# Attention worked in pairs of tiles, with k scaled behind the masks, gate sums behind the state products and expert 0's rows asked for earlier

## The chip, the cores and the metric

The kernel runs on one core of one Trainium2 chip. The metric is the device time of one launch in microseconds (us). The kernel before takes 944.06 us (median of 3 runs, 941.91 to 945.02).

## What is computed

Three layers follow one another. A causal attention with decay and without softmax runs over 4 sequences of 576 tokens, 8 heads of 64. A mixture of 8 experts, two per token, takes its output (2304 tokens of 512). A dense layer with a relu6 gate ends it.

```python
# attention, per head h:  gamma_h = 1 - 2**(-5-h)
scores = q @ k.T / sqrt(64)
ret    = scores * where(i >= j, gamma_h ** (i - j), 0)
x      = ret @ v                                     # (2304, 512)
# experts
noisy  = x @ w_gate + log1p(exp(x @ w_noise)) * noise
top2, weights = two largest of 8, softmax over the two
out[t] = sum over its two experts e of weight * relu(x[t] @ w1[e]) @ w2[e]
# dense
h = out @ w_in;  result = (h * clip(h + 3, 0, 6) / 6) @ w_out
```

## The kernel before

**Tiles.** The 2304 tokens are 18 tiles of 128 rows (`NT`), and a sequence is 4.5 tiles, so tile 4 of every nine (`m == 4`) holds the end of one sequence and the start of the next. The attention is linear in the past: a tile's output is the masked product of the tile with itself plus its queries times a state, the running sum of k^T v over the tiles before. One tile goes through these steps:

- `ks` (L196, VectorE) writes k divided by the decay at its position beside k; `qs` (L201, VectorE) scales the transposed q by a table.
- `tr` (L210, TensorE; L212, ScalarE) transposes the scaled k.
- `qk` (L226, TensorE) makes the scores of 8 heads in two PSUM banks, and VectorE multiplies each by the mask (L228, two instructions of 512 columns).
- `av` (L240) multiplies the state by q, `av2` (L250) adds the masked scores times v into the same PSUM tile `px`, and ScalarE copies `px` out in four pieces with a scale of its own for each (L267, eight pieces in tiles with `m == 4`).
- `kv` (L282) adds the tile to the state, and ScalarE copies the state out in one instruction (L284).
- `xt` (L294, L296) transposes the output back to rows for the scatter. For each three tiles `gsum` (L305, copy L307) makes the gate sums, `logit` (L313) folds them, and `route` turns them into slots.

**Order.** The order of every engine is written by hand; each engine runs its instructions in that order. The loop goes tile by tile: `xt(t-1)`, `tr(t+2)`, `av(t)`, `av2(t)`, `kv(t)`, then `ks` and `qs` of tile t+3, `qk(t+1)` with its masks, and `gsum` behind that. `route` is a generator; each `rstep()` runs one of its steps, five a tile. After its last step (L389) the slots of three tiles are known, and six scatters become ready.

**Scatter and rows.** Each `send` issues at most one scatter of a tile's rows to one of its two experts (a small spacer instruction, L412 or L414, and an indirect DMA, L415, both on GpSimd). `send` stands behind `tr`, `av2` and `xt`, so three a tile. At the end of tile 14 (`GA`) all scatters of tiles 0 to 11 (`EARLY` = 12) that are still open are issued at once, and `x_load` (L671) asks on the SP queue for expert 0's first 360 rows, which waits until every scatter has landed. In the last tile `x_tile` (L705) transposes these rows, and the first product of expert 0 (L738) follows the attention. Expert 0 runs in two sweeps (`si` 0 with 360 rows, `si` 1 with 256). In sweep 0 the rest of `route` and the last scatters run between the products; at its fifth step the slots are closed (`count`), the second load of expert 0's rows is asked for, and `fill` (L1265) marks unused slots of the other experts. Expert 1's rows are read (L683) behind the last `fill`, transposed by VectorE (L691), and expert 1 begins in sweep 2.

**PSUM.** The tag `acc` has five buffers, of which the state and the gate sums hold one each for good; `ga`, `gb` and `tp` have one each.

Of the kernel before, what the change touches and what calls it, by code (L numbers as in the profile page):

```python
# [7 lines left out]
F32 = mybir.dt.float32  # L8
F32R = mybir.dt.float32r
BF = mybir.dt.bfloat16  # L10
# [9 lines left out]
NT = N // 128  # L20
# [4 lines left out]
BZ = (7, 2)  # L25
# [12 lines left out]
C_ID, C_GK, C_GQ, C_MK, C_MM, C_IO, C_EB = 0, 128, 200, 272, 400, 528, 536  # L38
C_EC, C_FO, C_PI = 544, 552, 568
C_W = 569  # L40


def shape_consts():
    c = np.zeros((P, C_W + 320), np.float64)
    p = np.arange(P)
    c[:, C_ID:C_ID + P] = np.eye(P)
    le = (p[:, None] <= p[None, :]).astype(np.float64)
    c[:, C_MK:C_MK + P] = le
    c[:, C_MM:C_MM + P] = le * ((p[:, None] // 64) == (p[None, :] // 64))
# [4 lines left out]
    head = 2 * np.arange(4)[None, :] + (p // 64)[:, None]  # L54
    for m in range(9):
        c[:, C_GQ + m * 4:C_GQ + m * 4 + 4] = g[head] ** (m * P if m < 5 else m * P - S)
    c[:, C_GQ + 36:C_GQ + 40] = g[head] ** -64.0
# [22 lines left out]
class K:  # L80
# [32 lines left out]
    def consts(self):  # L113
        nc, cp, i = self.nc, self.cp, self.i
        nc.scalar.preload_act_table_set("natural_log_exp_and_others")
        self.c = cp.tile([P, C_W], F32, name="cst")
        nc.sync.dma_start(self.c[:, 0:C_MK], i["cst"][:, 0:C_MK])
        self.grow = self.big([P, 2048], BF)[0:6, 0:640]
        nc.gpsimd.dma_start(self.grow.bitcast(F32), i["cst"][0:6, C_W:C_W + 320])
        warm = self.row([P, 1024], BF)  # L120
        nc.vector.memset(warm, 0.0)
        self.warm = warm
        self.sbd = [self.row([P, 4, D]) for j in range(2)]
        self.ident = self.c[:, C_ID:C_ID + P]

    def table(self):

        nc = self.nc
        p = self.pacc([P, 512])
        nc.tensor.matmul(p, self.grow[:, 512:640], self.grow[:, 0:512], start=True, stop=True)  # L130
        self.gt = self.row([P, 512])
        nc.scalar.activation(self.gt, p, AF.Copy)

# [44 lines left out]
    def load(self, t, names="kqv"):  # L178
        nc, i = self.nc, self.i
        if t in self.raw:  # L180
            return self.load_of(t, names)
        kq = self.big([P, 2, H, D])
        vk = self.big([P, 2, H, D])
        self.raw[t] = dict(k=kq[:, 0], q=kq[:, 1], v=vk[:, 0], ks=vk[:, 1])
        self.load_of(t, names)
# [7 lines left out]
    def ks(self, t):  # L193
        m, r = t % 9, self.raw[t]
        gk = self.c[:, C_GK + m * 8:C_GK + m * 8 + 8]
        self.nc.vector.tensor_mul(r["ks"], r["k"], gk[:, :, None].to_broadcast([P, H, D]))  # L196
# [7 lines left out]
    def tr(self, t):  # L204
# [3 lines left out]
        sv = r["ks"].rearrange("p h d -> p (h d)")  # L208
        for a in range(4):
            nc.tensor.transpose(p[:, a, :], sv[:, a * P:(a + 1) * P], self.ident)  # L210
        r["kT"] = r["k"].rearrange("p h d -> p (h d)").rearrange("p (a i) -> p a i", a=4)
# [3 lines left out]
    def qk(self, t):  # L215
        nc = self.nc
        r = self.raw[t]
        mk = C_MM if t % 9 == 4 else C_MK
        mask = self.c[:, mk:mk + P]
        pt = self.big([P, 2, 4, P])  # L220
        p0 = self.ps.tile([P, 4, P], F32, name="sc0", tag="ga")
        p1 = self.ps.tile([P, 4, P], F32, name="sc1", tag="gb")
# [4 lines left out]
        for s, p in enumerate((p0, p1)):  # L227
            nc.vector.tensor_mul(pt[:, s], p, mask[:, None, :].to_broadcast([P, 4, P]))  # L228
        r["pt"] = pt

    def av(self, t):
        nc, m = self.nc, t % 9
        r = self.raw[t]
        px = (self.ps.tile([P, 2, P], F32, name="px", tag="tp"), self.pacc([P, 2, P]))
        n = 64 if m == 4 else P
        if m:
            for a in range(4):
                for u in range(2):
                    h, s = slice(u * 64, u * 64 + 64), u ^ a % 2
                    nc.tensor.matmul(px[a % 2][s * 64:s * 64 + 64, a // 2, :n], self.sbd[t % 2][h, a, :],  # L240
                                     r["qT"][h, a, :n], start=(a < 2), stop=False, skip_group_check=True)
        self.px = px

    def av2(self, t):
        nc, m = self.nc, t % 9
        r, px = self.raw[t], self.px
        for a in range(4):
            for s in range(2):
                h = slice(s * 64, s * 64 + 64)
                nc.tensor.matmul(px[a % 2][h, a // 2, :], r["v"][:, 2 * a + s, :], r["pt"][:, s ^ a % 2, a, :],  # L250
                                 start=(m == 0 and a < 2), stop=True, skip_group_check=True)
# [4 lines left out]
        w = self.c[:, C_GQ + m * 4:C_GQ + m * 4 + 4]  # L256
        if m == 0:
            for j in range(2):
                nc.scalar.activation(r["xT"][:, j::2], px[j], AF.Copy)
        elif t + 1 == NT:  # L260
            for j in range(2):
                nc.vector.tensor_mul(r["xT"][:, j::2], px[j],
                                     w[:, j::2, None].to_broadcast([P, 2, P]))
        else:
            n = 64 if m == 4 else P
            for a in range(4):
                nc.scalar.activation(r["xT"][:, a, :n], px[a % 2][:, a // 2, :n], AF.Copy, scale=w[:, a:a + 1])  # L267
                if m == 4:
                    nc.scalar.activation(r["xT"][:, a, n:], px[a % 2][:, a // 2, n:], AF.Copy, scale=self.c[:, C_GQ + 36 + a:C_GQ + 37 + a])
        self.send(r["xT"][:, 0])  # L270

    def kv(self, t):
# [7 lines left out]
        for h in range(H):  # L280
            a, s = divmod(h, 2)
            nc.tensor.matmul(self.pS[s * 64:s * 64 + 64, a, :], r["ks"][lo:, h, :], r["v"][lo:, int(HS[h]), :],  # L282
                             start=(m in (0, 4) and a == 0), stop=False, skip_group_check=True)
        nc.scalar.activation(self.sbd[(t + 1) % 2], self.pS, AF.Copy)  # L284

    def xt(self, t):
# [3 lines left out]
        if t == 0:  # L290
            self.pg = self.pacc([P, 512])
        p = self.pacc([P, 4, P])
# [6 lines left out]
    def gsum(self, g):  # L299

        nc = self.nc
        p = self.pacc([P, 3 * P])
# [6 lines left out]
    def logit(self, t):  # L309
        self.raw.pop(t)  # L310
        o = t % 8 * 16
# [5 lines left out]
    def route(self, g0, G):  # L317
        nc, sb, v = self.nc, self.sb, self.nc.vector
        lg = sb.tile([P, G, 16], F32, name="lg")
        for g in range(G):  # L320
            if g == 0 or (g0 + g) % 8 == 0:
                n = min(G - g, 8 - (g0 + g) % 8)
                o = (g0 + g) % 8 * 16
                v.tensor_copy(lg[:, g:g + n, :], self.pg[:, o:o + n * 16].rearrange("p (g e) -> p g e", g=n))
# [47 lines left out]
        o = 128 + g0 // 3 % 2 * 32  # L372
# [56 lines left out]
    def late_base(self):  # L429

        nc, cp, v = self.nc, self.cp, self.nc.vector
        p = self.pg[:, 192:200]
# [9 lines left out]
    def attention(self):  # L442
        self.raw, self.xrow, self.sq = {}, {}, []
        self.consts()
        self.load(0, "kq")
        self.load(1, "kq")
        self.nc.sync.dma_start(self.c[:, C_MK:], self.i["cst"][:, C_MK:C_W])
        self.load(0, "v")
        self.load(2, "kq")
        self.load(1, "v")  # L450
        self.load(3, "kq")
# [12 lines left out]
        self.tr(1)  # L464
        self.ks(2)
        self.qs(2)
        self.late_consts()
# [3 lines left out]
        for t in range(NT):  # L471
            if 0 < t < NT - 3:
                self.load(t + 3)
            if t in WL:
                self.w_load()
            self.rstep()

            if t:
                self.xt(t - 1)
                self.zero(t - 1)  # L480
            if 0 < t < NT - 2:
                self.tr(t + 2)
            if t and t % 3 == 0:
                self.gate(t - 1, groups)
            self.rstep()
            self.av(t)
            self.rstep()
            self.wstep(WM)

            self.av2(t)  # L490
            self.kv(t)
            if t == 0:
                self.tr(2)
            if t + 1 == NT:
                xs = self.x_new(0)
                self.x_tile(0, xs, 0, "acc")
                self.x_tile(0, xs, 1, "gb")
            self.rstep()
            if t + 3 < NT:
                self.ks(t + 3)  # L500
                self.qs(t + 3)

            if t + 1 < NT:
                self.qk(t + 1)
            if t % 3 == 2 and t + 1 < NT:
                self.gsum(t // 3)
            if t + 1 < NT:
                self.rstep()
# [7 lines left out]
            if t in WS:  # L516
                self.w_split()
            if t + 1 < NT:
                self.wstep(WN)
        self.gsum(NT // 3 - 1)  # L520
        self.x_tile(0, xs, 2, "tp")
        self.xt(NT - 1)
        self.gate(NT - 1, groups)
        self.rstep()
        self.wstep(WN)
# [915 lines left out]
```

## Time and profile before

| what | us |
|---|---|
| median of 3 runs | 944.06 |
| the profiled execution | 944.83 |
| its span, first to last instruction | 942.7 |
| TensorE busy in the span | 925.9 |
| VectorE busy | 612.6 |
| ScalarE busy | 466.4 |
| GpSimd busy | 238.5 |

The attention takes about the first 104 us of the span, the eight experts and the dense layer the rest. TensorE is busy 98% of the span. A profile gives for each instruction its start, its length and, where its engine was idle before it, what released it; lengths of TensorE instructions overlap, so a dense stretch is read from the distance of starts.

### The profile page before, as it was taken

To read this page: it belongs to the slowest core of one execution; us is meant where nothing else is said; L and a number is where in the kernel's file an instruction comes from. 1 tells how busy PE (TensorE), PEld (TensorE's weight loads), DVE (VectorE), ACT (ScalarE), POOL (GpSimd) and SP (SyncE) were. 2 spreads that over 40 slices of the span, in tenths; PEclk is the share of its full clock that TensorE was granted. 3 is DMA by queue.
4 is the path that set the end of the run, shared out by engine and by line. 5 is a ranking of instruction groups with operands and counts; after the bars stand their busy time and mean duration, and the time that the engine had idled before them with its cause. 6 is when DMAs were issued, how large, how long until landed. Compare 5 with 4: busy or idle time off the path is not lost.

```text
span 942.7 us, 17785 instructions
## 1 busy us (share of the span) xinstructions
PE 925.9 (98%) x6314; PEld 819.6 (87%) x6314; DVE 612.6 (65%) x1327; ACT 466.4 (49%) x1025; POOL 238.5 (25%) x324
## 2 busy tenths in 40 slices
PE   8998999999999999999999999999999999999997
PEld 6876888988888989888888888989999999899996
DVE  5776765887979888796866536645645554574442
ACT  4655543556464564645535435544545454445342
POOL 1246260433324242332500213033004212400000
PEclk9999999999999999999999999999999999999999
DMA  9963766767969788696657678778579676956541
GB/s 336 376 236 126 278 211 231 234 220 253 291 218 292 246 262 251 209 271 210 200 179 244 231 264 295 265 244 262 183 254 286 207 229 235 275 188 214 179 157 49
DMA packets 123742, 221.22 MB, mean 235 GB/s; under 512 B 13037, under 2 KB 60915, under 8 KB 123643
## 3 DMA queue, kind: packets, MB, share of 16 engines
q1 hardware_dynamic: 113819, 190.47, 61.6%
q0 software_dynamic: 9392, 28.73, 8.9%
q8 instruction: 52, 0.85, 0.4%
q10 hardware_dynamic: 432, 0.79, 0.2%
q14 instruction: 47, 0.39, 0.1%
HBM read 163.97 MB, written 55.97 MB: 233 GB/s over the span
## 4 chain that ended last, share of the span: by engine, by line
PE 87%; DVE 4%; DMA 2%; ACT 2%; issue 2%; POOL 1%; SPq 1%; another core or an unknown queue 0%; DVEq 0%; ACTq 0%; POOLq 0%
PE p L755 40%; PE ga L738 12%; PE gb L738 9%; PE mga L1167 7%; PE p L1167 5%; PE mgb L1167 2%; PE mtp L1167 2%; PE sc L226 2%; PE px L250 1%; DVE b L592 1%; PE p L294 1%; PE p L210 1%; PE p L282 1%; ACT b L591 1%; DMA xe<-s,free 1%
## 5 line engine op out<-in xcount | busy, mean ns | idle before, releaser
L755 PE MATMUL p<-b,h 128*120 128x512 f32 (+1 forms) x1056 | 261.0, 395 | 0.0
L755 PEld LDWEIGHTS p<-b,h 128*120 128x120 f32 (+1 forms) x1056 | 189.1, 185 | 41.5 <-DVE h L797 0.4
L755 PE MATMUL p<-b,b 128*128 128x512 f32 x768 | 180.0, 390 | 0.0
L755 PEld LDWEIGHTS p<-b,b 128*128 128x128 f32 x768 | 142.2, 188 | 28.2
L738 PE MATMUL ga<-x,b 128*128 128x360 f32 (+1 forms) x768 | 134.2, 323 | 2.1 <-DVE h L797 1.9
L738 PEld LDWEIGHTS ga<-x,b 128*128 128x128 f32 x768 | 124.8, 188 | 10.8 <-DVE h L797 6.4
L641 POOL TENSOR_TENSOR cvl<-cvl,cvs 128x256 f32<-128x256 f32 x64 | 50.4, 787 | 214.9 <-ACT cva L622 150.8
L592 DVE TENSOR_TENSOR b<-b,b 128x512 fp32r<-128x512 f32 x128 | 93.6, 766 | 13.9 <-ACT b L591 13.6
L738 PE MATMUL gb<-b,b 128*128 128x256 f32 x672 | 89.8, 282 | 0.1
L738 PEld LDWEIGHTS gb<-b,b 128*128 128x128 f32 x672 | 86.9, 190 | 1.4 <-DVE b L694 0.3
L884 POOL DMA_INDIRECT s<-yd,slotc x36 | 37.3, 1037 | 179.6 <-DVE b L1030 56.1
L591 ACT ACTIVATE b<-b 128x512 fp32r<-128x512 f32 x128 | 74.0, 625 | 0.0
L1205 DVE SCALAR_TENSOR_TENSOR b<-s,b 128x512 fp32r<-128x512 f32 x64 | 44.3, 693 | 44.9 <-ACT b L1204 40.5
L1204 ACT ACTIVATE b<-s 128x512 fp32r<-128x512 f32 x64 | 40.5, 632 | 59.3 <-DVE s L1202 53.1
L642 POOL TENSOR_TENSOR cvl<-cvt,cvl 128x256 f32<-128x256 f32 x64 | 59.2, 925 | 5.0
L1201 ACT ACTIVATE s<-s,three 128x512 f32<-128x512 f32 x64 | 45.8, 716 | 25.4 <-DVE s L1188 25.4
L1167 PE MATMUL mga<-b,b 128*128 128x256 f32 x384 | 56.2, 282 | 0.0
L797 DVE SCALAR_TENSOR_TENSOR h<-gb,h 128x256 fp32r<-128x256 f32 (+1 forms) x64 | 27.8, 434 | 43.4 <-PE p L755 30.6
L1188 DVE TENSOR_TENSOR s<-p,mc 128x256 f32<-128x256 f32 x32 | 13.6, 424 | 64.4 <-PE p L1167 64.0
L1167 PEld LDWEIGHTS mga<-b,b 128*128 128x128 f32 x384 | 52.6, 191 | 2.5
L1202 DVE SCALAR_TENSOR_TENSOR s<-s,s 128x512 f32<-128x512 f32 x64 | 44.0, 687 | 7.4 <-DMA paced<-s 4.6
L1172 ACT ACTIVATE mc<-mga 128x256 f32<-128x256 f32 x64 | 24.5, 383 | 48.3 <-PE mga L1167 47.1
(206 smaller groups left out, 1440.1 us busy)
## 6 DMA issues: line engine op xcount, KB each, us to landing
b<-wc SPq DMA_DIRECT2D x112, 512.0 KB
b<-in_moe_w_dram SPq DMA_DIRECT2D x64, 512.0 KB
wc<-b SPq DMA_DIRECT2D x32, 512.0 KB
s<-xe SPq DMA_DIRECT2D x140, 64.0 KB
s<-in_moe_w_in_dram SPq DMA_DIRECT2D x32, 256.0 KB
s<-in_moe_w_out_dram SPq DMA_DIRECT2D x32, 256.0 KB
b<-wc SPq DMA_DIRECT2D x32, 256.0 KB
yd<-s SPq DMA_DIRECT2D x24, 240.0 KB
```

Source lines behind the costliest of these rows:

```text
L591: self.nc.scalar.activation(h, a, AF.Copy)
L592: rest = lambda h=h, l=l, a=a: self.nc.vector.tensor_sub(l, a, h.bitcast(F32))
L641: nc.gpsimd.tensor_mul(lf, lf, s.bitcast(F32))
L642: nc.gpsimd.tensor_add(lf, t.bitcast(F32), lf)
L738: nc.tensor.matmul(p, a[k], b[:, k, :n], start=(i == 0), stop=(i == 11))
L755: nc.tensor.matmul(a[:R], x[:, c], y[:, fi, :], start=(first and i == 0), stop=(last and i == 2))
L884: nc.gpsimd.indirect_dma_start(out=r, out_offset=None, in_=self.yd[0:rows], in_offset=bass.IndirectOffsetOnAxis(ap=self.slotc[:, t, k:k + ...
L1167: nc.tensor.matmul(t, w[:, u, k], x[:, z, k], start=(first and i == 0), stop=(last and i == 5), skip_group_check=True)
L1201: nc.scalar.activation(r, x, AF.Relu, bias=self.three)
L1202: v.scalar_tensor_tensor(x, r, 6.0, x, op0=OP.min, op1=OP.mult)
L1204: nc.scalar.activation(h[:, 0], x, AF.Copy, scale=1.0 / 6.0)
L1205: v.scalar_tensor_tensor(h[:, 1], x, 1.0 / 6.0, h[:, 0].bitcast(F32), op0=OP.mult, op1=OP.subtract)
```

## The change

- The loop goes over pairs of tiles. In a pair t: `kv(t+1)`; `av2` of both tiles; one copy of both tiles' `px` for each of its two halves (`px_out`, ScalarE, without a scale; four copies where the two tiles fall in different groups of three); `kv(t+2)`; `qk` and masks of t+2 and t+3; `ks(t+3)`; `av` of t+2 and t+3; `gsum` if a group of three has ended; `xt` of t and t+1; `tr` of t+4 and t+5; `gate`; `qs` of both and `ks(t+4)`. Nine `rstep()`s stand in a pair.
- The decay between tiles is applied to the state where it is copied out (four ScalarE instructions of 64 columns with a scale each, instead of one of 256).
- `tr` transposes the raw k. `ks` then scales k in place, and the masks carry the factor (`dm`, made at the start by two VectorE instructions of 512 columns).
- The scores of odd tiles use the tag `acc`, the row transposes of `xt` the tags `ga` and `gb`; the gate sums share the bank of the logits.
- At the start the small table of decays is asked for on ScalarE's queue instead of GpSimd's, the order of the first loads is another, and the warming matmuls are 6, 4 and 2 instead of 7 and 2.
- The forced scatters and `x_load` stand at the start of pair 14, and the first two steps of the loop (tile 0's and 1's scores) stand ahead of it.

```diff
     def av(self, t):
+        if t % 2 == 0 or t == 1:
+            self.px = (self.ps.tile([P, 2, 2, P], F32, name="px", tag="tp"), self.pacc([P, 2, 2, P]))
...
+    def px_out(self, t):
+        for j in range(2):
+            if t % 3 == 2:
+                for u in (t, t + 1):
+                    nc.scalar.activation(self.raw[u]["xT"][:, j::2], self.px[j][:, u - t], AF.Copy)
+                continue
+            x = self.xg[t // 3][:, j::2, c:c + 2 * P].rearrange("p a (t i) -> p a t i", t=2)
+            y = self.px[j].rearrange("p t a i -> p a t i")
...
+                nc.scalar.activation(x, y, AF.Copy)
+        for u in (t, t + 1):
+            self.send(self.raw[u]["xT"][:, 0])
...
     def kv(self, t):
-        nc.scalar.activation(self.sbd[(t + 1) % 2], self.pS, AF.Copy)
+        w = C_GQ + (t + 1) % 9 * 4
+        for a in range(4):
+            nc.scalar.activation(self.sbd[(t + 1) % 2][:, a], self.pS[:, a], AF.Copy, scale=self.c[:, w + a:w + a + 1])
...
         self.busy(BZ[0])
         self.table()
-        self.ks(0)
         self.tr(0)
+        self.decays(0)
         self.qs(0)
-        self.ks(1)
+        self.decays(1)
+        self.busy(BZ[1])
         self.qs(1)
-        self.busy(BZ[1])
-        self.qk(0)
+        sc = self.qk(0)
         self.gate_w()
         self.tr(1)
+        self.ks(0)
+        self.masks(0, *sc)
+        self.busy(BZ[2])
+        sc = self.qk(1)
+        self.kv(0)
+        self.tr(2)
+        self.ks(1)
+        self.masks(1, *sc)
+        self.av(1)
+        self.tr(3)
...
+        for t in range(0, NT, 2):
+            last = t + 2 == NT
...
             if t == GA:
                 while self.sent < EARLY:
                     self.rstep()
                     self.send()
                 self.xr = {}
                 self.x_load(0, 0)
...
+            self.rstep()
+            self.kv(t + 1)
+            self.rstep()
+            self.av2(t)
+            self.av2(t + 1)
+            self.px_out(t)
+            if last:
+                xs = self.x_new(0)
+                self.x_tile(0, xs, 0, "acc")
+                self.x_tile(0, xs, 1, "gb")
+            else:
+                self.kv(t + 2)
+                self.rstep()
                 self.wstep(WN)
+                for u in (t + 2, t + 3):
+                    self.masks(u, *self.qk(u))
+                self.ks(t + 3)
+            self.rstep()
...
+            if not last:
+                self.av(t + 2)
+                self.av(t + 3)
+            if done:
+                self.gsum(g)
+            if last:
+                self.x_tile(0, xs, 2, "tp")
+            for u in (t, t + 1):
+                self.xt(u)
+                self.zero(u)
+            for u in (t + 4, t + 5):
+                if u < NT:
+                    self.tr(u)
+            if done:
+                self.gate(3 * g + 2, groups)
+            if t + 4 < NT:
+                self.qs(t + 4)
+                self.qs(t + 5)
+                self.ks(t + 4)
+            for _ in range(4):
+                self.rstep()
...
+            self.wstep(WN)
+            self.rstep()
```

## Rows read from the trace of the kernel before

**Rows 1.** The page's first part: busy time and share of each engine.

```profile
PE 925.9 (98%) x6314; PEld 819.6 (87%) x6314; DVE 612.6 (65%) x1327; ACT 466.4 (49%) x1025; POOL 238.5 (25%) x324
```

**Rows 2.** Busy time by stretch: window, length, engines, TensorE clock, DMA share, GB/s.

```profile
20.00:30.00 10.00, 10.00 (x174) 8.39 (x168) 6.15 (x15) 6.27 (x19) 0.00 (x0) 1.00 1.03 376
60.00:70.00 10.00, 9.15 (x144) 7.49 (x145) 9.62 (x36) 6.61 (x19) 3.65 (x6) 1.00 0.24 91
```

**Rows 3.** Chain of work to 200 us, pieces of TensorE: start us, us, what.

```profile
17.57 1.09 PE sc L226 x16
...
21.77 1.09 PE sc L226 x16
...
24.23 0.44 PE p L210 x4
...
25.84 0.37 PE px L250 x4
...
40.16 0.37 PE px L250 x4
...
54.97 0.37 PE px L250 x4
...
61.14 0.32 PE px L250
...
81.94 0.37 PE px L250 x4
```

**Rows 4.** Timeline of the start, TensorE, then VectorE: start us, us, instruction, [idle before].

```profile
1.48 3.17 PE L138 MATMUL p<-s 128*128 128x512 bf16 x7 [1.48 <-DVE s L121]
5.35 0.60 PE L130 MATMUL p<-b 6*128 6x512 bf16 x1 [0.70 <-DMA b<-in_cst_dram]
...
7.78 2.07 PE L226 MATMUL sc<-b 64*128 64x128 f32 x16
...
6.62 0.69 DVE L201 TENSOR_TENSOR b<-b,s 128x512 f32<-128x512 f32 x1 [1.77 <-ACT s L132]
```

**Rows 5.** Timeline of GpSimd's scatters, 74 to 91 us.

```profile
74.03 1.26 POOL L415 DMA_INDIRECT xe<-s,slots  x1 [0.15 <-issue]
...
78.74 1.25 POOL L415 DMA_INDIRECT xe<-s,slots  x1 [0.16 <-issue]
...
85.36 0.97 POOL L415 DMA_INDIRECT xe<-s,slots  x1 [0.22 <-issue]
...
90.86 0.97 POOL L415 DMA_INDIRECT xe<-s,slots  x1 [0.23 <-issue]
```

**Rows 6.** Timeline of SP's queue, then TensorE, around expert 0's first rows.

```profile
93.85 1.37 SPq L671 DMA_DIRECT2D s<-xe  x3
98.71 0.22 SPq L515 DMA_DIRECT2D paced<-s  x1
...
101.14 0.63 PE L705 MATMUL p<-cst,s 120*128 120x120 f32 x4
...
103.11 0.63 PE L705 MATMUL xp<-cst,s 120*128 120x120 f32 x4
...
104.60 0.58 PE L738 MATMUL ga<-x,b 128*128 128x360 f32 x2
```

**Rows 7.** Timeline of all engines, last scatters to the first product of expert 1.

```profile
117.77 0.97 POOL L415 DMA_INDIRECT xe<-s,slots  x1 [3.65 <-ACT h L796]
...
117.81 0.53 DVE L797 SCALAR_TENSOR_TENSOR h<-gb,h 128x360 fp32r<-128x360 f32 x1 [0.81 <-ACT h L796]
...
127.57 0.82 SPq L671 DMA_DIRECT2D s<-xe  x2
...
131.68 1.10 POOL L1265 DMA_INDIRECT xe<-s,free  x1 [5.79 <-DVE b L592]
...
150.79 0.73 DVE L691 STREAM_TRANSPOSE xp<-s 128x512 f32<-128x512 f32 x1 [2.70 <-DMA s<-xe]
...
160.70 2.25 PE L738 MATMUL ga<-x,b 128*128 128x360 f32 x12 [0.53 <-DVE h L797]
```

More of the change, by code (lines that the diff above doesn't have):

```diff
@@ L24 @@
 EARLY = 12
-BZ = (7, 2)
+BZ = (6, 4, 2)
 WL, WS = (9, 11, 13, 15), (10, 14)
@@ L217, in qk @@
         r = self.raw[t]
[L218 to L219 removed]
         pt = self.big([P, 2, 4, P])
[L221 to L222 removed]
+        p0, p1 = (self.pacc([P, 4, P]) if t % 2 else self.ps.tile([P, 4, P], F32, name="sc", tag=tag) for tag in ("ga", "gb"))
         for a in range(4):
@@ L226, in qk, with masks @@
                 nc.tensor.matmul(p[:, a, :], r["kT"][h, a, :], r["qT"][h, a, :], start=True, stop=True)
-        for s, p in enumerate((p0, p1)):
-            nc.vector.tensor_mul(pt[:, s], p, mask[:, None, :].to_broadcast([P, 4, P]))
-        r["pt"] = pt
+        return pt, (p0, p1)
+    def masks(self, t, pt, ps):
+        nc = self.nc
+        for s, p in enumerate(ps):
+            nc.vector.tensor_mul(pt[:, s], p, self.dm[:, s])
+        if t % 9 == 4:
+            nc.vector.memset(pt[0:64, :, :, 64:P], 0.0)
+        self.raw[t]["pt"] = pt
     def av(self, t):
@@ L233, in av @@
         r = self.raw[t]
-        px = (self.ps.tile([P, 2, P], F32, name="px", tag="tp"), self.pacc([P, 2, P]))
+        if t % 2 == 0 or t == 1:
+            self.px = (self.ps.tile([P, 2, 2, P], F32, name="px", tag="tp"), self.pacc([P, 2, 2, P]))
+        px = [x[:, t % 2] for x in self.px]
+        first = t % 2 == 0 or t % 9 == 1
         n = 64 if m == 4 else P
@@ L240, in av @@
                     nc.tensor.matmul(px[a % 2][s * 64:s * 64 + 64, a // 2, :n], self.sbd[t % 2][h, a, :],
-                                     r["qT"][h, a, :n], start=(a < 2), stop=False, skip_group_check=True)
-        self.px = px
+                                     r["qT"][h, a, :n], start=(first and a < 2), stop=False, skip_group_check=True)
     def av2(self, t):
         nc, m = self.nc, t % 9
-        r, px = self.raw[t], self.px
+        r, px = self.raw[t], [x[:, t % 2] for x in self.px]
         for a in range(4):
@@ L250, in av2 @@
                 nc.tensor.matmul(px[a % 2][h, a // 2, :], r["v"][:, 2 * a + s, :], r["pt"][:, s ^ a % 2, a, :],
-                                 start=(m == 0 and a < 2), stop=True, skip_group_check=True)
+                                 start=False, stop=True, skip_group_check=True)
         g = t // 3
@@ L255, in av2 @@
         r["xT"] = self.xg[g][:, :, t % 3 * P:t % 3 * P + P]
[L256 to L270, printed above, removed]
+    def px_out(self, t):
+        nc = self.nc
+        r, c = self.raw[t], t % 3 * P
+        for j in range(2):
[5 more added lines that the diff above has]
+            y = self.px[j].rearrange("p t a i -> p a t i")
+            if j and t + 2 == NT:
+                nc.vector.tensor_copy(x, y)
+            else:
+                nc.scalar.activation(x, y, AF.Copy)
+        for u in (t, t + 1):
+            self.send(self.raw[u]["xT"][:, 0])
     def kv(self, t):
@@ L319, in route @@
         lg = sb.tile([P, G, 16], F32, name="lg")
[L320 to L324, printed above, removed]
+        v.tensor_copy(lg, self.pg[:, 0:G * 16].rearrange("p (g e) -> p g e", g=G))
         yield
@@ L444, in attention @@
         self.consts()
[L445 to L451, printed above, removed]
+        for t, nm in ((0, "kq"), (1, "kq"), (0, "v"), (2, "k"), (3, "k"), (1, "v"), (2, "q"), (3, "q")):
+            self.load(t, nm)
+        self.nc.sync.dma_start(self.c[:, C_IO:], self.i["cst"][:, C_IO:C_W])
         self.load(2, "v")
@@ L470, in attention @@
         self.live, self.sent, self.xg = [], 0, {}
[L471 to L508, printed above, removed]
+        self.pg = self.pacc([P, 512])
+        for t in range(0, NT, 2):
+            last = t + 2 == NT
+            for u in (t, t + 1):
+                if u + 4 < NT:
+                    self.load(u + 4)
+                if u in WL:
+                    self.w_load()
             if t == GA:
```

64 lines of the change are left out of this document (32 added, 32 removed).

## The prediction, made before the changed kernel was run

> **What bounds the kernel now.** I read the page's busy shares first: TensorE has work for 925.9 of 942.7 us [rows 1]. So the change can gain only what TensorE idles in the attention: it moves the time at which the first product of expert 0 starts, 104.60 [rows 6], and any wait it makes later. Then the windows: at 20 to 30 us TensorE is full and VectorE has 6.15 of 10; at 60 to 70 VectorE is at 9.62 and TensorE falls to 9.15 [rows 2]. Then the chain, for distances. From the scores of one tile to those of the next (17.57 to 21.77) are 4.20: a plain tile. From `av2` of tile 3 (25.84) to that of tile 6 (40.16) are 14.32 [rows 3]: three tiles (12.6) and 1.7 for a group's gate sums, logits and routing. From tile 9 (54.97) to tile 10 (61.14) it took 6.17 [rows 3], 1.97 over a plain tile, in the stretch in which VectorE is full: `av2` waits for masks that have little other work ahead of them. Last I read GpSimd and SP, since slots, scatters and the request for rows form a chain beside TensorE.
>
> **Part A, the start.** Before, the decay table arrives at 5.35, after 0.70 of idle TensorE; `qs(0)` waits for it until 6.62 and the first scores start at 7.78 [rows 4]. On ScalarE's queue I expect it when six warming matmuls end (seven took 3.17): 1.48 + 6 x 0.45 = 4.2; at worst, if that queue is no faster, at 5.35 as before. The scores then wait for the transposed k and for up to four more warming matmuls (1.8 at the same pace): 6.8 to 7.3. The masks' factor, two VectorE instructions of 0.69 [rows 4], lies where VectorE waited for the table (1.77 idle there); without that cover it would cost 1.4. Now count to equal work: `qk(2)` begins at 17.57 [rows 3], behind the scores, masks and states of tiles 0 and 1. Of a plain tile's 4.20, `qk` is 1.09, `tr` 0.44 and `xt` about 0.5 [rows 3]; `av` is 0.6 (what lies from the end of `tr` to 25.84, less 0.6 for `logit`), so `av2` and `kv` are 1.6. Behind the first scores stand `qk(1)` 1.1, three `tr` 1.4, `av2` and `kv` twice 3.2, `av(1)` 0.6, two warming matmuls 0.5 and about 0.5 of waiting for the first state: 7.3. The first scores end at 7.9 (at 1.09) to 9.4 (at the 2.07 of [rows 4]), so this ends at 15.2 to 16.7, and `xt(0)`, 0.5, is still owed. Gain 0.4 to 1.9; I take 1.3.
>
> **Part B, the loop up to pair 14.** Every matmul stays. What goes is the wait of `av2` for masks, which now stand a whole pair ahead: 1.97 at tile 9 and, by the same subtraction at tiles 10 and 12, perhaps 0.7 more: 2.7. Fewer changes of matmul shape (eight a pair for twelve) may give another 0.1 a pair. What comes: VectorE's masks and scalings are eight instructions of at most 0.69 a pair, 5.5; where routing and weight splits come on top, two tiles fill VectorE with 9.6 [rows 2], as much as TensorE's 8.4 to 9.5 for a pair. There, in pairs 10 and 12, VectorE still binds and 0 to 2 come back. On ScalarE the copies of `px` fall from eight to two a pair and those of the state rise from two to eight; the trace shows no state copy with a scale, but in a pair they have the scores ahead of the next `av` as cover, 2.2; if ScalarE is late by more than that, each pair pays the rest. The odd tile's scores hold two `acc` buffers that `tr(t+4)` needs; `av`, `xt` and the even tile's masks lie between, about 1 us of room. `ks(t+4)` now waits for that `tr`; behind it on VectorE stand only routing steps. Sum: a gain of 2.5, between 4.4 and a loss of 0.5. With A, pair 14 starts 3.8 sooner. The same work (`kv(14)`, `qk(15)`, `av(15)`, `tr(17)` done) stands before at 81.94 [rows 3] plus 0.6 + 1.1 + 0.6 + 0.4 = 84.6; now 80.8.
>
> **Part C, from there to the first product of expert 0.** Before: 104.6 - 84.6 = 20.0. TensorE's own work in the new order is 8.4 + 1.3 - 0.9 = 8.8 for pair 14 (gate work added, no `tr`), 2.0 for the last two `av2`, then 101.14 to 104.60 [rows 6] and a second `xt`, 4.0: 14.8. It will not run so, since the rows come later. Counting routing steps (11 a group, nine a pair), the slots of tiles 6 to 8 are ready only at the end of pair 10, those of tiles 9 to 11 at the end of pair 12. So pair 12 issues six scatters and the start of pair 14 forces six more, back to back. GpSimd needs (78.74 - 74.03)/3 = 1.6 for one that waits for a tile's copy and (90.86 - 85.36)/4 = 1.4 for a forced one [rows 5]. Two go out before `xt(12)`; four follow from 1.2 ahead of pair 14 (5.3 at 1.3 each to 7.0), then six (8.2): the last ends 12.3 to 14.0 after pair 14 starts. Before, the last ended at 91.83 (90.86 + 0.97), the request followed 2.0 later (93.85), and the third tile of rows was there 4.8 after that (98.71) [rows 5, 6]. So now it is there at 19.1 to 20.8; its transpose, two `xt` and `logit` (103.11 to 104.60 [rows 6], and 0.5) end at 21.1 to 22.8. Against 20.0 that costs 1.1 to 2.8; I take 1.9. TensorE, ready for the rows at 10.8, would wait some 6. Asking sooner does not help: the scatters are what is late. SP is not: the fourth weight load now stands ahead of the request.
>
> **Part D, expert 1.** By the same count the last group's slots come at the first routing step of step 3 of sweep 0, not at the end of step 2. On VectorE that lies behind the instruction at 117.81, so its six scatters start near 119.3, not 117.77 [rows 7]. Behind them follow the second request of expert 0's rows (127.57), `fill` (131.68, which must not overtake that read), and expert 1's rows, for which VectorE waits 2.70 until 150.79 and TensorE 0.53 at 160.70 [rows 7]. So the chain has no slack: 1.6 goes in, of which VectorE may make up half over five tiles of rows. Cost 0 to 1.6; I take 0.8.
>
> **Sum.** -1.3 - 2.5 + 1.9 + 0.8 = -1.1 on the profiled 944.83. That execution is 0.8 over the median, so the median goes from 944.06 to 943.0. The four terms will not all fall on one side: 939.5 to 947 for this case.
>
> **Rivals.** (1) The rows are in time: the scatters do not queue as I count, and part C is 14.8 plus 1 of small waits, 4.2 less than before: -1.3 - 2.5 - 4.2 + 0.8 = -7.2, 937. For it: GpSimd is busy 3.65 of 10 at 60 to 70 [rows 2]. Against: twelve scatters at 1.4 to 1.6 need 18, two pairs. (2) Slower: a wait of 6 for the rows lowers TensorE's clock, and what follows runs at half speed. The granted clock reads 1.00 in both windows [rows 2], the level of 2.4 GHz; but the first scores took 2.07 for what takes 1.09 later [rows 3, 4], as at 1.2 GHz. The 4 behind the wait would take up to 4 more: 943.0 + 4 = 947. [...] The Trainium skill, "TensorE: Matmul & The Clock Gate" (Part 1), has the array start at 1.2 GHz and fall back to it when it has idled; the start agrees, and no wait of before is long enough to show the fall. (3) VectorE binds all pairs and B is a loss of 1.4: 946.9. For it: 9.62 at 60 to 70; against: 6.15 at 20 to 30 [rows 2].
>
> **How the numbers follow.** A difference under 0.3% (2.8) can't be told from none. Forecast 0.53, rival 1 0.19, rival 2 0.18, rival 3 0.10. Faster (below 941.2): rival 1 and 0.08 of the forecast's low end, 0.27. Slower (above 946.9): half of rivals 2 and 3 and 0.08 of the high end, 0.22. Same: 0.51. The range takes in the forecast's bounds, rival 3, most of rival 2 and the upper part of rival 1: 938.5 to 947.5.
>
> **What would show it.** After: the table before 4.5 and first scores near 7; no idle TensorE ahead of `av2`; ten scatters in a row around pair 14; a long idle stretch of TensorE ahead of the first transposes of expert 0's rows, ended by that load, with the first product near 102.7; doubled lengths behind it for rival 2. VectorE's first transpose for expert 1 stands 47 to 48 behind that product, not 46.2. I am wrong if TensorE goes through the last pair without a wait (rival 1), or if the pairs themselves stall.

## The result, and the profile after

The changed kernel takes 957.31 us (median of 4 runs, 956.41 to 958.46). The kernel before, run beside it on the same chip, takes 943.71 (941.91 to 945.02). The ratio is 1.0146, 95% interval [1.0126, 1.0167]: 13.6 us slower, where 943.0 was forecast and 947.5 was the upper end.

The profiled execution took 956.41, its span is 954.2. First the page's busy times, which answer [rows 1]:

```profile
PE 929.6 (97%) x6317; PEld 823.1 (86%) x6317; DVE 613.8 (64%) x1328; ACT 466.3 (49%) x1024; POOL 236.2 (25%) x323
```

TensorE's busy time rose by 3.7 only, the span by 11.5. Before, the first product of expert 0 started at 104.60 [rows 6]; now it starts at 115.20, 10.6 later, and behind it lie 839.0 where 838.1 lay before. So the loss is in the attention. The windows of that stretch, after (columns as in [rows 2]):

```profile
50.00:60.00 10.00, 8.14 (x98) 5.43 (x95) 4.16 (x9) 2.61 (x11) 4.60 (x8) 0.83 0.92 311
60.00:70.00 10.00, 8.29 (x118) 7.36 (x116) 4.94 (x26) 6.12 (x19) 4.67 (x8) 1.00 0.56 183
70.00:80.00 10.00, 7.26 (x133) 6.22 (x133) 8.04 (x24) 5.50 (x16) 0.00 (x0) 1.00 0.10 36
90.00:100.00 10.00, 6.28 (x44) 4.10 (x43) 0.00 (x0) 2.14 (x8) 8.46 (x16) 0.70 0.56 211
```

From 90 to 100 TensorE ran 44 matmuls (174 in the full window of [rows 2]), VectorE no instruction at all, ScalarE was busy for 2.14 and GpSimd for 8.46. The timeline of after, TensorE, then VectorE, GpSimd and SP's queue (columns as in [rows 4]):

```profile
4.15 0.60 PE L128 MATMUL p<-b 6*128 6x512 bf16 x1
...
6.41 1.16 PE L228 MATMUL sc<-b,b 64*128 64x128 f32 x16
...
15.43 1.16 PE L228 MATMUL sc<-b,b 64*128 64x128 f32 x16
...
87.06 0.69 PE L294 MATMUL p<-b,b 128*64 128x64 f32 x16
...
94.27 0.61 PE L228 MATMUL p<-b,b 64*128 64x128 f32 x3
95.69 1.11 PE L228 MATMUL p<-b,b 64*128 64x128 f32 x5 [0.80 <-issue]
97.13 0.78 PE L228 MATMUL p<-b,b 64*128 64x128 f32 x3 [0.34 <-issue]
98.54 0.81 PE L228 MATMUL p<-b,b 64*128 64x128 f32 x4 [0.63 <-issue]
...
110.28 0.83 PE L317 MATMUL p<-x,wgn 128*32 128x384 f32 x2 [1.13 <-ACT x L280]
111.73 0.85 PE L317 MATMUL p<-x,wgn 128*32 128x384 f32 x6 [0.62 <-DVE x L278]
...
101.59 1.29 DVE L234 TENSOR_TENSOR b<-sc,b 128x512 f32<-128x512 f32 x2 [11.80 <-PE p L228]
...
87.01 1.18 POOL L423 DMA_INDIRECT xe<-s,slots  x1 [0.44 <-ACT s L308]
...
99.01 0.96 POOL L423 DMA_INDIRECT xe<-s,slots  x1 [0.22 <-issue]
...
101.79 1.41 SPq L692 DMA_DIRECT2D s<-xe  x3
106.72 0.22 SPq L500 DMA_DIRECT2D paced<-s  x1
```

The start is as forecast (table at 4.15, scores at 6.41 and at full pace). Pair 14 begins at 87.06, not at 80.8. Ten scatters stand in a row, as forecast. TensorE begins to stall some 3 us into the row, and from 94 until 100, when the last scatter has ended, it gets three to five matmuls per 1.4 us, waiting for nothing that the profile shows ("issue"). VectorE's next masks read scores that were finished when the row at 94.27 began, and start at 101.59, 7.3 later. TensorE never waits for the rows; it is later than they are.

### The profile page after: what moved, and what is told of

Read it like the earlier page. It is cut to its first block, busy times and chain, and to the rows that moved or that the text cites. A ratio compares the mean times of both kernels' runs of the same rounds, so it can differ in the third digit from the quotient of the medians.

```text
span 954.2 us, 17781 instructions
## 1 busy us (share of the span) xinstructions
PE 929.6 (97%) x6317; PEld 823.1 (86%) x6317; DVE 613.8 (64%) x1328; ACT 466.3 (49%) x1024; POOL 236.2 (25%) x323
## 5 line engine op out<-in xcount | busy, mean ns | idle before, releaser
L1209 DVE TENSOR_TENSOR s<-p,mc 128x256 f32<-128x256 f32 x32 | 13.6, 425 | 63.4 <-PE p L1188 61.0
L818 DVE SCALAR_TENSOR_TENSOR h<-ga,h 128x360 fp32r<-128x360 f32 (+1 forms) x64 | 32.8, 512 | 22.3 <-ACT h L817 22.2
```

The costliest lines, as they stand in the source:

```text
L818: nc.vector.scalar_tensor_tensor(hl, p, 0.0, hh.bitcast(F32), op0=OP.max, op1=OP.subtract)
```

## The experiments

Kernels were run in five further sessions, each on one chip, the kernel before beside them. That kernel came out at one of two levels: 933.7 to 934.0 in three sessions, 942.7 and 943.5 in two, and 944 for the prediction. Times are compared inside a session; I write "at 934" and "at 944". What sets the level stays open. The number of the chip alone does not: of two sessions on chip number 2 one was at 934 and one at 944. Where the quoted expectations say "first" and "second chip", read 944 and 934.

**Scatters left out, at 934.** Plain copies of the same bytes for the 24 scatters of tiles 0 to 11, on SP's and on GpSimd's queue; expert 0 takes its rows from these copies.

```diff
-        st = nc.gpsimd.indirect_dma_start(...)
+        if t >= EARLY: st = nc.gpsimd.indirect_dma_start(...)
+        else: st = nc.sync.dma_start(self.xe[r:r + P], self.xrow[t])   # second kernel: nc.gpsimd
```

> The changed kernel, with the 24 scatters of tiles 0 to 11 replaced by plain copies of the same rows (256 KB each) on SP's queue to fixed places, and with the experts' rows read from there (the experts get rows by position, not by slot). GpSimd keeps only its spacers in the attention. In the changed kernel's trace TensorE runs out of instructions ('issue' gaps after every 4 to 5 matmuls, at 52 to 56, 65 to 68 and 89 to 101 us), each time some us into a row of back-to-back scatters (44 to 55, 62 to 67, 86 to 100). Theory 1, the row of scatters on GpSimd's queue starves TensorE: no such gaps, the first product of expert 0 near 97 to 100 instead of 115.2, time 938 to 944. Theory 2, the denser order of the pairs outruns TensorE's issue by itself: the gaps stay, time 953 to 958.

> As the one with rows on SP's queue, but the plain copies stay on GpSimd's queue: same bytes, same queue, no list of rows. If it is any back-to-back DMA work of GpSimd that starves TensorE, the issue gaps stay at 52 to 56 and 89 to 101 us and the time is 950 to 958. If it is the indirect form alone, it is like the kernel with SP's queue, 938 to 944. Theory 2 (order of the pairs): 953 to 958.

Measured: 937.4, ratio 1.0039 [1.0026, 1.0052], and 937.27, 1.0036 [1.0022, 1.005]. No gap put down to issue is there. That says nothing of the scatters yet, since at 934 the changed kernel has none either (its own run is below). But both are slower than before: the pairs have waits of their own, without any row being late.

**A train of scatters in the kernel before, at 934.** The twelve scatters of tiles 0 to 5 were to be held back and issued in a row; in the program they stand together behind tile 8.

> The kernel before, tile by tile, but with the 12 scatters of tiles 0 to 5 held back until the end of tile 8 and issued back to back (about 60 to 76 us); all else as before. Theory 1: TensorE shows issue gaps of 0.3 to 0.9 us some 4 to 8 us into this row of scatters, 3 to 8 us in all, time 946 to 951. Theory 2: no more gaps than in the kernel before, time within 2 us of it.

Measured: 933.37, ratio 0.9994 [0.9984, 1.0003], no gap. But the train of twelve never came about. Moved together, the scatters lost the spacers that wait for the tiles, and GpSimd issued them as soon as slots were known, six from 34.20 to 41.33 and six from 48.42 to 55.22:

```profile
41.33 0.97 POOL L415 DMA_INDIRECT xe<-s,slots  x1 [0.23 <-issue]
48.42 1.27 POOL L415 DMA_INDIRECT xe<-s,slots  x1 [6.03 <-ACT x L267]
```

All it shows is that at 934 six in a row cost nothing; it could not decide.

**Scatters spread, two more routing steps a pair, at 934:**

> The changed kernel with its six scatters of a pair spread over the pair (behind the state copy, the px copy, each tile's masks, one xt and one tr) and two more routing steps a pair, so that the last slots come earlier and fewer scatters are forced; all is computed. Theory 1: with about 1 us between scatters the gaps shrink; first product of expert 0 at 98 to 108, time 940 to 950. Theory 2: 953 to 958.

Measured: 944.63, 1.0118 [1.0101, 1.0134], no better than the changed kernel itself at this level (next run). TensorE waits 3.16 for the rows, and 1.49, 2.30 and 2.01 for VectorE.

**The changed kernel at 934.** This separates its own cost from the stalls.

> The changed kernel as it is, beside the kernel before on the chip of this call. Theory 1 (most of the loss is TensorE standing in 'issue', its instructions trickling, while rows are scattered, and how much depends on the chip): where the kernel before shows such gaps (944 on the first chip) this one shows more and stands some 13 above it; where it shows none (933.7 on the second chip) this one stands only 4 to 9 above it, by the wait for the state's copy (2.5), by the last gate sum (1.75) and by the rows (0 to 4). Rival (the order itself is what costs 13, through waits on ScalarE and VectorE): 12 to 14 above on any chip.

Measured: 943.8, ratio 1.0104 [1.0088, 1.0119]: 10.0 slower, a little over what I had allowed, and by another way than at 944. TensorE's timeline, then SP's queue:

```profile
71.47 0.69 PE L294 MATMUL p<-b,b 128*64 128x64 f32 x16 [2.51 <-ACT s L298]
...
78.89 0.69 PE L294 MATMUL p<-b,b 128*64 128x64 f32 x16
...
97.24 1.06 PE L726 MATMUL p<-cst,s 120*128 120x120 f32 x4 [8.13 <-DMA s<-xe]
98.24 1.03 PE L726 MATMUL xp<-cst,s 120*128 120x120 f32 x4
...
104.11 2.22 PE L759 MATMUL ga<-x,b 128*128 128x360 f32 x12
...
94.24 1.41 SPq L692 DMA_DIRECT2D s<-xe  x3
99.17 0.22 SPq L500 DMA_DIRECT2D paced<-s  x1
```

And the windows of the same run:

```profile
80.00:90.00 10.00, 9.11 (x161) 7.85 (x155) 6.11 (x20) 5.69 (x18) 8.41 (x17) 1.00 0.49 186
90.00:100.00 10.00, 2.76 (x16) 1.58 (x16) 3.07 (x12) 1.85 (x4) 2.29 (x4) 0.66 0.46 154
98.00:102.00 4.00, 4.00 (x21) 2.25 (x20) 2.00 (x12) 1.89 (x4) 0.00 (x0) 0.50 0.44 134
100.00:110.00 10.00, 10.00 (x68) 8.96 (x61) 6.58 (x28) 5.34 (x13) 1.33 (x3) 0.83 0.93 307
```

Here is the wait for the rows, 8.13, and behind it the granted clock at 0.50 from 98 to 102: the four transposes take 1.06, not 0.63 [rows 6]. No gap put down to issue stands from 12 to 110. In the same session:

> The changed kernel with the 24 scatters of tiles 0 to 11 replaced by plain copies on the same queue, and expert 0 reading rows from there (its values are not the reference's). Theory 1: no issue gaps on any chip; 3 to 4 above the kernel before where that shows none, and level with it or below where that has 5 or 6 us of gaps. Rival (the chip's fetch of instructions is slow whatever is scattered): as many gaps as the changed kernel on the same chip.

Measured: 936.89, 1.0034 [1.0022, 1.0046]. The first product starts at 95.81, 8.3 sooner. So at 934, some 7 of the 10 are late rows and the clock behind them, and 3.1 are the rest of the change.

> The changed kernel with the decay table asked for on GpSimd's queue again, as before: one piece of part A undone. By part A the table arrives about 1.2 later (5.35 for 4.15), the first scores start about 1.0 to 1.2 later, and the time is 1.0 to 1.2 above the changed kernel. Rival (a later wait takes the gain away): within 0.5 of it.

The table back on GpSimd's queue: 946.42, ratio 1.0129 [1.0109, 1.0149], 2.6 over the changed kernel, not 1.0 to 1.2; but the two intervals overlap, and by their times alone the two are not told apart. In the trace the table came 0.19 later only, and the first scores ran at half pace:

```profile
4.34 0.60 PE L128 MATMUL p<-b 6*128 6x512 bf16 x1
4.87 1.11 PE L216 MATMUL p<-cst,b 128*128 128x128 f32 x4
5.78 1.91 PE L144 MATMUL p<-s 128*128 128x512 bf16 x4
7.62 2.08 PE L228 MATMUL sc<-b,b 64*128 64x128 f32 x16
```

The scores of tile 1 start at 11.44, where the changed kernel has them at 9.17. I take the half pace for the lower clock because three kinds of instruction show it at once (1.11, 1.91 and 2.08 for 0.66, 1.03 and 1.16 in the changed kernel); the column of the granted clock reads 1.00 there, so only the lengths say it.

**The pairs' own waits, at 934.** The splits of weights moved behind the scores and masks, off ScalarE's way to the state's copy:

```diff
-                self.wstep(WN)
                 for u in (t + 2, t + 3):
                     self.masks(u, *self.qk(u))
                 self.ks(t + 3)
+                self.wstep(2 * WN)
...
-            self.wstep(WN)
+            if last:
+                self.wstep(WN)
```

> The changed kernel with the two weight splits of a pair's end moved behind the next pair's scores and masks, so that they no longer stand on ScalarE ahead of the state's copies and of px_out. Theory (ScalarE late, as part B's condition said): the wait of TensorE for the state's copy near pair 12 (2.55 where plain copies stood for the scatters) falls below 1 and that of the last gate sum (1.13 and 0.62) below 0.6, so 2 to 4 us below the changed kernel, unless the rows are then waited for. Rival (the waits are the pair's own order, not the splits): less than 1 us.

> The changed kernel with plain copies for the 24 scatters (as in the run with plain copies on GpSimd's queue, which stood 3.1 to 3.5 above the kernel before) and with the pair's weight splits moved behind the next scores and masks. Theory (pairs bunch VectorE's work too: with the splits moved, routing is late by 2.3 instead of the state's copy by 2.5): 1 to 2 less than with plain copies alone, so 1 to 3 above the kernel before. Rival (ScalarE's order is the whole of it): 3.5 to 4.5 less, level with the kernel before or under it.

Measured: 942.8, ratio 1.0099 [1.0085, 1.0114], beside 943.8 of the changed kernel; TensorE still waits 4.21 for the rows. With plain copies as well 936.83, 1.003 [1.0021, 1.0039], beside 1.0034 with plain copies alone, in another session. TensorE's timeline in the second of them:

```profile
70.44 0.69 PE L294 MATMUL p<-b,b 128*64 128x64 f32 x16 [0.82 <-ACT s L298]
...
78.30 0.17 PE L386 MATMUL p<-ra,tri 128*128 128x8 bf16 x1 [2.26 <-DVE ra L374]
```

The wait for ScalarE shrinks from 2.54 to 0.82, and the one for VectorE's routing grows from 0.46 to 2.26: the splits' second half is VectorE's. The time stays.

**The wait filled with warming matmuls, at 934:** `self.busy(36)` behind the last `px_out`.

> The changed kernel with 36 warming matmuls (some 7.7 us at full clock, results unused) put where TensorE waits 8.13 for expert 0's rows. Theory (rival 2 of the prediction: the wait lowers the clock, and what stands behind the rows runs at half pace, 6.87 from the rows to the first product where 4.0 would do): the granted clock stays at 1.00 from 80 to 110 us, the first product starts some 2.9 earlier, the time is 2 to 3.5 below the changed kernel. Rival (the work behind the rows is slow because it waits for ScalarE and VectorE, not for the clock): within 0.7 of it.

Measured: 942.97, 1.0091 [1.0075, 1.0106]; next to 1.0104 that can't be told apart. In the trace the clock stays at 1.00 from 80 to 110, and from the arrival of the rows to the first product it is 4.89 (98.04 to 102.93), not 6.87: 2.0 come back where I had expected 2.9, since waits of 0.28 and 0.40 appear. That the clock fell because of the wait is shown: with the wait filled it did not fall. What that is worth in the time is not shown.

**The kernel before, its trace at 934:**

> The kernel before, unchanged, to have its trace on the chip of this call. Part B of the prediction took the 6.17 from av2 of tile 9 to av2 of tile 10 (1.97 over a plain tile) for a wait on masks, because VectorE is full there. Theory now (that stretch was TensorE standing in issue while rows were scattered): on a chip where this kernel takes 934 the two are 4.2 to 4.6 apart, TensorE is busy 9.9 of 10 at 60 to 70 us with VectorE at 9.0 or more, and the first product of expert 0 starts near 93 to 95. Rival (VectorE binds there): 5.5 to 6.2 apart on any chip.

Measured: 934.28. TensorE's timeline with `av2` of tiles 9 and 10, then of tile 14, and the first product of expert 0:

```profile
52.54 0.44 PE L250 MATMUL px<-b,b 128*64 128x128 f32 x4
...
56.74 0.44 PE L250 MATMUL px<-b,b 128*64 128x128 f32 x4
...
75.96 0.44 PE L250 MATMUL px<-b,b 128*64 128x128 f32 x4
...
94.93 2.23 PE L738 MATMUL ga<-x,b 128*128 128x360 f32 x12
```

The same two points in the trace of the prediction:

```profile
54.90 0.44 PE L250 MATMUL px<-b,b 128*64 128x128 f32 x4
...
60.55 0.43 PE L250 MATMUL px<-b,b 128*64 128x128 f32 x2 [1.12 <-DVE b L228]
```

And the window in which VectorE is fullest, beside a full TensorE:

```profile
60.00:70.00 10.00, 10.00 (x161) 8.46 (x160) 9.22 (x26) 7.59 (x22) 3.79 (x6) 1.00 0.21 80
```

At 934 they are 4.20 apart, a plain tile, in the trace of the prediction 5.65. (The 6.17 of the prediction ends at 61.14, which is a later product of tile 10's `av2`, not its first.) At 934 TensorE waits for another engine from 20 to 110 us only 0.47 and 0.17.

**Part A alone, at 934:** the kernel before with the table on ScalarE's queue and six warming matmuls for seven.

> The kernel before with the start's part alone: decay table asked for on ScalarE's queue, six warming matmuls for seven. Part A alone: the table at 4.2, first scores 0.5 to 1.2 sooner at full pace, all of it kept, because TensorE is full behind it: 0.5 to 1.3 below the kernel before, and 2 to 3 where the clock would have risen late. Rival (loads or masks are late next): within 0.4.

Measured: 933.12, ratio 0.9992 [0.9982, 1.0001]. 0.8 sooner, which could still be nothing; it is not shown to beat the kernel before. Part of the reason is that the kernel before does not always start at half pace: in two other traces of its start, unchanged, the first scores begin at 6.54 and 6.31 and take 1.16 (the train of scatters, and the copies in the kernel before).

**At 944 again.** The changed kernel, and one whose scatters go to slots known from the start, so that no routing holds them:

```diff
+        nc.gpsimd.iota(self.slotk, pattern=[[P, EARLY], [REG, 2]], base=CAP, channel_multiplier=1)
...
-   ... IndirectOffsetOnAxis(ap=self.slots[:, t, k:k + 1], axis=0)
+   ... IndirectOffsetOnAxis(ap=(self.slotk if t < EARLY else self.slots)[:, t, k:k + 1], axis=0)
```

> The changed kernel once more, on the chip of this call. Where the kernel before takes 934 here: 9 to 11 above it, with a wait for expert 0's rows of 7 to 9 and the granted clock below 0.9 in the windows around 90 to 110. Where the kernel before takes 944: 13 to 14 above it, with windows before 90 in which neither TensorE nor VectorE is busy.

> The changed kernel with the 24 scatters of tiles 0 to 11 sent to slots that are known from the start (expert 0 reads its rows from there, so its values are not the reference's), each as soon as its tile's rows are copied: same indirect scatters, same queue, no routing ahead of them. Theory (part C: slots are late, and six forced scatters behind them; scatters cost nothing besides): no wait for rows, 3 to 4 above the kernel before, as with plain copies. Rival (indirect scatters slow the pairs by themselves): 5 or more above it, though the rows are in time.

Measured: 955.97, ratio 1.0142 [1.0124, 1.0159], the first result again; and 958.38, 1.0158 [1.0135, 1.0181]. In the second, the scatters pile up elsewhere, and the stall goes with them. They do not go out as soon as their rows are copied: GpSimd waits for earlier writes into the same buffer (up to 5.73 us, at 40.75), and then issues sixteen in a row from 67.25 to 88.00. The windows of that run:

```profile
50.00:60.00 10.00, 9.89 (x176) 8.59 (x174) 7.11 (x21) 6.55 (x23) 2.68 (x4) 1.00 0.16 62
...
70.00:80.00 10.00, 6.25 (x45) 4.16 (x45) 3.48 (x20) 2.66 (x8) 8.90 (x15) 0.69 0.91 312
80.00:90.00 10.00, 6.31 (x24) 2.78 (x25) 2.68 (x4) 2.06 (x7) 8.13 (x14) 0.50 0.81 322
90.00:100.00 10.00, 9.93 (x148) 9.36 (x151) 6.55 (x18) 5.35 (x16) 0.00 (x0) 0.79 0.56 190
```

And TensorE's timeline in it:

```profile
81.50 0.46 PE L253 MATMUL px<-b,s 64*64 64x128 f32 x1 [0.36 <-issue]
82.90 0.37 PE L253 MATMUL px<-b,s 64*64 64x128 f32 x1 [0.94 <-issue]
83.61 0.37 PE L253 MATMUL px<-b,s 64*64 64x128 f32 x1 [0.34 <-issue]
```

From 50 to 60, where the changed kernel stalled among scatters, there is only one and TensorE is full; at 80 to 90 it gets 24 matmuls, all at half clock. Two more routing steps a pair, alone and with the splits moved:

> The changed kernel with two more routing steps at the end of each pair (11 in a pair for nine), so that the slots of tiles 6 to 11 are there most of a pair sooner. Theory (slots late): the wait for rows falls by 3 to 6 and the time by 3 to 6, less what TensorE then waits for VectorE's routing (the run with six scatters spread had 5 of that). Rival (the pace of the scatters alone sets the rows): wait and time within 1.5 of the changed kernel.

> Two more routing steps a pair and the weight splits moved behind the scores and masks, together. Theory (each of the pair's engines is late in turn, so the mends do not add up): 3 to 6 above the kernel before. Rival (the two mends add up): level with it or below.

Measured: 965.5, 1.024 [1.0218, 1.0263], and 962.63, 1.0206 [1.0187, 1.0224]: worse, and beyond every figure I had written. In the first of them TensorE waits from 35 us on, 2.51 for the state's copy, 1.33 and 1.64 for VectorE. The twelfth scatter starts sooner, at 61.99 (65.17 in the changed kernel), but the last of the 24 at 106.69 (98.25). More routing in a pair made the last slots later, not sooner.

**The decision, at 944.** Plain copies in both kernels:

> The kernel before with its 24 scatters of tiles 0 to 11 replaced by plain copies of the same bytes on the same queue (expert 0 reads its rows from there, so its values are not the reference's). Theory (indirect scatters in a row keep TensorE and VectorE from their next instructions, on some chips): on a chip where the kernel before takes 943 this one takes 934 to 937, and its trace has no gaps put down to issue from 40 to 95; where the kernel before takes 934, within 1 of it. Rival (the stalls come with the bytes or with the chip, not with the scatters): within 2 of the kernel before on either chip, gaps included.

> The changed kernel with the same replacement. Theory: 937 to 941 on either kind of chip, 3 to 4 above the run of the kernel before with plain copies; no issue gaps. Rival (bytes or chip): 950 or more where the kernel before takes 943.

Measured, with the kernel before at 943.48: before with copies 933.74, ratio 0.9898 [0.9883, 0.9912], 0.3 under the range that I gave; after with copies 938.82, 0.9958 [0.9943, 0.9973], 5.1 over the kernel before with copies where I gave 3 to 4. No gap put down to issue is left in the trace of the kernel before with copies. The software queue carries the same in the kernel before with and without copies, 9392 packets and 28.73 MB. The windows of the kernel before with copies, the second of which was at 9.15 in [rows 2]:

```profile
50.00:60.00 10.00, 10.00 (x160) 8.72 (x152) 8.10 (x33) 6.54 (x19) 3.46 (x10) 1.00 1.00 374
60.00:70.00 10.00, 10.00 (x167) 8.46 (x170) 9.22 (x26) 7.47 (x22) 3.45 (x8) 1.00 0.42 142
```

The gap between the two levels, 9.7 in the kernel before, is the indirect scatters. It isn't their bytes, nor the waiting for slots, which the run with fixed slots had taken away without gain in the changed kernel. It isn't the rows' places either: the fixed slots were the very rows that the copies write. And it isn't the load of the DMA engines: TensorE is full here beside a DMA share of 1.00, and stalls beside 0.56 at 90 to 100 in the changed kernel. One more thing does change with the form: GpSimd is busy 0.54 us with a copy, and 0.96 to 1.5 with a scatter. In the changed kernel copies bring 955.97 less 942.68 (13.3 over before) down to 5.1 over the kernel before with copies.

## Why the prediction was wrong

**Part A** held in the trace: table 4.15 for 4.2, scores 6.41 against 6.8 to 7.3, and the scores of tile 2 at 15.43 for 17.57 [rows 3], 2.1 sooner, so 1.6 less the 0.5 still owed (1.3 forecast). In part this is luck. With the queue undone the table came at 4.34, not at 5.35, so the queue itself was worth 0.19. The worth is mostly whether the first scores run at half pace, which [rows 4] showed as 2.07 for 1.09 and I did not price: with the queue undone tile 1 came 2.3 later.

**Part B** is the step that failed. With part A as it came, the loop lost 4.1 up to pair 14, where I had a gain of 2.5. I read the 1.97 over a plain tile at tile 10 as a wait for VectorE, because a window starting there had VectorE at 9.62 [rows 2, 3]. The window was right, the place was not. TensorE's scores of tile 10, and VectorE's rows just ahead of their masks, before:

```profile
56.38 1.16 PE L226 MATMUL sc<-b 64*128 64x128 f32 x16
...
57.16 0.69 DVE L201 TENSOR_TENSOR b<-b,s 128x512 f32<-128x512 f32 x1
59.80 1.29 DVE L228 TENSOR_TENSOR b<-sc,cst 128x512 f32<-128x512 f32 x2 [1.95 <-PE p L210]
```

VectorE stood idle 1.95, with its scores done since 57.54. TensorE, VectorE, ScalarE and GpSimd were busy 2.59, 2.06, 1.58 and 2.12 of the 4 us from 58 to 62. Nobody bound that stretch; it was a stall beside scatters, and at 934 it is gone. So there was no 2.7 of masks to win. And the stalls grew: part C counted the scatters in a row and what they do to the rows, but put nothing down for the engines beside them. What scatters cost is 9.7 in the kernel before and some 18 in the changed one (13.3 + 9.7 - 5.1 by the last two sessions, with all that comes of them). Pair 14 starts 6.3 later than forecast (87.06 for 80.8). (The terms of part B as they stand add up to 1.5 to 3.5; its wider bounds, 4.4 and -0.5, have no terms.)

What pairs do save I put at 0.1 a pair. At 934 with copies (the run beside the changed kernel), `av2` of tile 0 to `av2` of tile 2 is 7.74 (12.97 to 20.71), against 8.40 for two plain tiles. Over eight pairs it is 73.84 (12.97 to 86.81), of which 4.25 are waits, so 69.6 against 74.4 before (scores of tile 1 to those of tile 17, 12.64 to 87.04). That stretch holds one `kv` and one `tr` less in the pairs, 1.0 together, so the pairs gain some 3.8 of TensorE's time. They pay back more in waits: 2.54 for the state's copy, 0.78 for masks and 0.93 for routing, then 1.13 and 0.62 at the last gate sum and 0.40. My condition ("if ScalarE is late by more than that") came true at 2.5, once and not in each pair (at 944 too, 2.74 in the first trace): ScalarE's copies stand behind two weight splits and behind a logarithm that waits 0.93 for VectorE.

**Part C**, at 934, was right to the row, counted from the start of pair 14 at 78.89: last scatter ended 13.5 behind it (12.3 to 14.0 forecast), request at 94.24, third tile of rows at 99.17, so 20.3 behind it (19.1 to 20.8). The wait was 8.13 (some 6). From the pair to the first product it took 25.2, not 21.1 to 22.8; the excess is mostly the half clock, 6.87 for 4.0 behind the rows, of which the filled wait brought 2.0 back. That is **rival 2**, mechanism and sign, which I gave 0.18 and added as 4 to a gain that did not exist. By the Trainium skill, "TensorE: Matmul & The Clock Gate" (Part 1), the array goes back to 1.2 GHz when it has idled; the trace agrees, a granted clock of 0.50 behind 8.13 of idling. At 944 the wait could not appear: stalls made TensorE later than the rows, while from 90 to 100, with matmuls a few at a time, the granted clock read 0.70.

**Part D** held in its number: 0.9 for 0.8, and VectorE's first transpose for expert 1 stands 47.69 behind the first product (47 to 48). The last group's scatters stand 2.5 later behind that product than before (130.91 - 115.20 against 117.77 - 104.60), not 1.6, so more was made up than the half that I allowed.

**Rival 1** is ruled out by the copies: with rows in time the pairs are 3 to 5 slower, not 7 faster. **Rival 3** has the wrong cause: VectorE is at 9.2 beside a full TensorE.

The terms, from the profiled runs (at 944 the first two traces; at 934 the traces of before and after there, with the same points, from two sessions):

| term | forecast | at 944 | at 934 |
|---|---|---|---|
| A and B: equal work against the start of pair 14 | -3.8 | 87.06 - 84.6 = +2.5 | 78.89 - 78.7 = +0.2 |
| C: from there to the first product | +1.9 | 28.1 - 20.0 = +8.1 | 25.2 - 16.2 = +9.0 |
| D: the rest of the span | +0.8 | +0.9 | +0.9 |
| sum | -1.1 | +11.5 | +10.1 |

(78.7 is 75.96, where `av2` of tile 14 starts at 934, and the prediction's 2.7 behind it; 16.2 is from there to 94.93.)

## What to carry to other kernels

Before a gap is put down to an engine, look whether that engine was busy in the gap itself; a window of ten microseconds mixes the stall with the catching up behind it. A gap in which all engines stand with their inputs ready is a resource of its own: find what runs in it (here scatters), and ask whether the change makes that run longer in a row. Bunching steps saved TensorE time here (0.66 on a plain pair; that it is the changes of shape is argued, not shown), but it bunches the other engines' work as well, and moving one late step let the next one be late.

## What the runs showed of the hardware

At one of the two levels, indirect scatters issued in a row by GpSimd kept TensorE, VectorE and ScalarE from starting instructions whose inputs were ready. In the changed kernel VectorE began its masks 7.3 us after their scores were done, and ScalarE began its copy of `px` at 93.55, 4.1 us after the last product of `av2`; with fixed slots TensorE got 24 matmuls in 10 us. Plain copies of the same bytes on the same queue did not, and took 9.7 us off the kernel before. Through which path (the fetching of instructions, semaphores, or another) no run here shows. A fetch under way is not what TensorE waited for: no packet of an instruction queue moved from 93.3 to 101.3 in the changed kernel, nor from 91.5 to 104 when it was run again, nor from 80.5 to 91 with fixed slots. The Trainium skill, "Runtime: NRT & Kernel Launch" (Instruction fetch mechanics), calls the cost of fetching the next block mostly hidden; no run here shows these stalls to be that cost.

TensorE's clock, once down, stayed down while matmuls came a few at a time. In the run with fixed slots it fell behind a wait of 2.53 for the state's copy and read 0.50 from 74 to 94, though no idle time of TensorE there was longer than 0.94. So a wait of 2.5 can cost more than itself, though not each time: in the changed kernel at 934 the same wait (2.51) was followed by scores of 1.60 and 1.92 at a granted clock of 0.66 and 0.50, with plain copies (2.54) by scores of 1.16 at 1.00.
